# The values' scaling by the lengths of K: one VectorE instruction in the middle of a chunk step, or eight ScalarE instructions at its end

## The chip, the cores and the metric

One core of one Trainium2 chip runs the whole program. The metric is the device time of one execution in microseconds (us). Three runs of the kernel before are at hand, and one further execution with the profiler on, from which all rows below are taken.

## What is computed

Three stages follow one another: linear attention with the delta rule over 4 x 8 heads of 768 tokens and 48 features, then a mixture of 8 experts over 3072 tokens, then a gated feed-forward layer. The change lies in the first stage.

```python
k_n = k / (norm(k, axis=-1) + 1e-06)
for t in range(S):
    y[:, :, t] = einsum('bhd,bhde->bhe', q[:, :, t], state)
    v_old = einsum('bhde,bhd->bhe', state, k_n[:, :, t])
    state = state + beta[:, :, t] * einsum('bhd,bhe->bhde', k_n[:, :, t], v[:, :, t] - v_old)
```

## The kernel before

The attention works in 24 chunk steps (NSTEP) of 32 tokens, all 32 heads at once: 128 partitions hold 4 batches x 32 tokens, and the 8 heads lie along the free axis. Four steps make a group g, so there are six groups. K is used unnormalized in two products, and to make up for that the values V of a step are multiplied by the lengths of K, which stand in `nt` (one number per partition and head). `v_mul` (L203) does that in place on the tile VT, two steps ahead of the use; from step 1 on it is called with VectorE (L893). Steps 0 to 2 got theirs from GpSimd earlier.

In a step TensorE's work stands in this order: KS (the state read with K), Y's first half (the state read with Q), U (a triangular inverse times W), XTP (transposes of the step before for the gate of the experts), 24 of the 32 matmuls GP (K with K and Q with K, eleven steps ahead, only while there are such steps, s <= 12), Sps (the new state), Y's second half, GL (the gate), and the last 8 of GP. Between them stand these hand-overs: VectorE makes W from VT and KS (L804); U waits for W; ScalarE copies U to UH in half precision (L830), VectorE subtracts that to get the low half (L834); Sps waits for UH, behind its first 16 of 48 matmuls also for the low half; ScalarE copies Sps to SH, from which the next step's KS is read.

ScalarE's queue at a step's end holds: the evacuation XG of Y (L502), in every second step a cast PHL (L291), the copies G and P of GP (L272), then `kh_mul` (L301, eight activations ks, one per head, each with a column of `rnt` as its scale, in the form that the changed `v_mul` has too), in every second step the two casts KH (L314), in some steps a zeroing of X, and then, in the next step, two copies of the inverse into TBD (L401) in four steps of the attention, and UH.

VectorE has besides a background work: for every group the inverse of a 32x32 triangular matrix per head is made column by column (tiles X, tmp, Lt), and ends with a transpose XT and the copies into TBD. An object `Filler` (L96) deals this work out while the program is written. It keeps a clock of its own, and `run(budget)` (L123) places background instructions until the budget is used up; `spend(dur)` (L129) moves the clock on by what other VectorE work takes, so that less background work is placed. Each step has a budget of TA = 3.4 between U and UH and TB = 6.8 at its end (TC = 5.8 once s + 1 + LA >= NSTEP, with LA = 11). The transpose XT of group g + 1 may come from step 4g on (`limit`, L837). The engines' queues keep the order of the program (class Queue, L75): an instruction that waits holds up all behind it on its engine.

Where this text says step s, it means the stretch from UH of step s to UH of step s + 1, and W(s), U(s), UH(s) are the instructions of step s.

Of the kernel before, what the change touches and what calls it, by code (L numbers as in the profile page):

```python
# [12 lines left out]
AF = mybir.ActivationFunctionType  # L13
# [8 lines left out]
NSTEP, NG = SEQ // CH, SEQ // CH // 4  # L22
# [119 lines left out]
class Attention:  # L142
# [5 lines left out]
    def run(self, small, acc, zero_fill, small_loads):  # L148
        tc, a, beside = self.tc, self.a, self.beside
        nc = tc.nc  # L150
        V, A, G = [Queue(tc, e) for e in (nc.vector, nc.scalar, nc.gpsimd)]
# [15 lines left out]
        nt = cp.tile([128, NG, 32], F32, name="nt")  # L167
# [35 lines left out]
        def v_mul(s, E=G):  # L203
            g, s4 = divmod(s, 4)
            norms(g)
            v = VT[s // 2][:, s % 2].rearrange("p (h e) -> p h e", h=8)
            E.tensor_tensor(out=v, in0=v, in1=nt[:, g, 8 * s4 : 8 * s4 + 8].unsqueeze(2).to_broadcast([128, 8, 48]), op=ALU.mult)


# [2 lines left out]
        def gp_mm(s, hs, mm=T.matmul):  # L212
            if s not in GPS:
                tag = {4: "KS", 5: "Y", 7: "XTP", 8: "GL", 9: "U"}.get(s, "GP")
                GPS[s] = pool(tag).tile([128, 8, 64], F32, tag=tag, name="GP", bufs=1)
            ps, t = GPS[s], KT[s]
            for h in hs:
                for p in range(2):
                    mm(out=ps[64 * p : 64 * p + 64, h], lhsT=KB[s % RK][0:112, p, :, h], rhs=t[0:112, :, p, :, h], start=True, stop=True)
# [45 lines left out]
        def gp_evac(s):  # L265

            ps = GPS.pop(s)
            KT.pop(s)
            g, s4 = divmod(s, 4)
            if s4 == 0 and g > 0:  # L270
                GPM[g] = [ep.tile([128, 32, 32], F32, tag=n, name=n, bufs=b) for n, b in (("G", 2), ("P", 2))]
            A.copy(out=GPM[g][0][:, 8 * s4 : 8 * s4 + 8], in_=ps[:, :, 0:32])  # L272
            return A.copy(out=GPM[g][1][:, 8 * s4 : 8 * s4 + 8], in_=ps[:, :, 32:64]).ins
# [4 lines left out]
        def p_split(u, E=G):  # L278
            g, i = divmod(u, 2)
            if g:  # L280
                norms(g)
                pm = GPM[g][1][:, 16 * i : 16 * i + 16]
                E.tensor_tensor(out=pm, in0=pm, in1=rnt[:, g, 16 * i : 16 * i + 16].unsqueeze(2).to_broadcast([128, 16, 32]), op=ALU.mult)
            else:
                pm = PM.pop(u)
            E.tensor_tensor(out=pm, in0=pm, in1=mask.unsqueeze(1).to_broadcast([128, 16, 32]), op=ALU.mult)
            PHL[u] = wk.tile([128, 2, 16, 32], F16, tag="PHL", name="PHL", bufs=4)
            PMS[u] = pm
# [7 lines left out]
        def expand(dst, src):  # L296
            for b in range(4):
                SP.dma_start(out=dst[32 * b : 32 * b + 32, :, :, b].rearrange("p a k i -> p (a k) i"), in_=src[32 * b : 32 * b + 32].rearrange("p a k i -> p (a k) i"))


        def kh_mul(u, half=None):  # L301
            norms(u // 2)
            r = rnt[:, u // 2].rearrange("p (s h) -> p s h", s=4)
            if u not in KS_N:
                KS_N[u] = wk.tile([128, 2, 8, 48], F32, tag="ks", name="ks", bufs=1)
            for i in (range(2) if half is None else (half,)):
                for h in range(8):
                    A.activation(out=KS_N[u][:, i, h], in_=KTOK[u][:, i, :, h], func=AF.Copy, scale=r[:, 2 * (u % 2) + i, h : h + 1])

        def kh_split_hi(u):  # L310
            KTOK.pop(u)
            KH = wk.tile([128, 2, 2, 8, 48], F16, tag="KH", name="KH", bufs=1)
            for s in range(2):
                A.copy(out=KH[:, s, 0], in_=KS_N[u][:, s])  # L314
            KHG[u] = KH
# [67 lines left out]
        def norms(g):  # L383
            while g not in normed:
                fil.step()
# [112 lines left out]
        def x_evac(s, Yp):  # L498
            if s % 2 == 0:
                XGP[s // 2] = gs.tile([128, 2, ROW], F32, tag="XG", name="XG", bufs=4)  # L500
            XG[s] = XGP[s // 2][:, s % 2]
            A.activation(out=XG[s][:, 0:384], in_=fl(Yp), func=AF.Copy, scale=1.0 / SIG)  # L502
# [98 lines left out]
        def scatter(s):  # L601
            g, s4 = divmod(s, 4)
            pos, sc = GT[g]
            x = XG.pop(s)
            G.tensor_copy(out=x[:, 384:386], in_=sc[:, s4])
            r = G.indirect_dma_start(out=self.disp, out_offset=bass.IndirectOffsetOnAxis(ap=pos[:, s4 : s4 + 1], axis=0), in_=x, in_offset=None)
            if s >= NSTEP - 8:

                tc.declare_no_dep(r.ins, group=f"rows{g}", reason="each token has a row of its own")
                tc.add_to_no_dep_group(f"rows{g}", r.ins)  # L610
# [26 lines left out]
        fil = Filler()  # L637
# [49 lines left out]
        for ops in prep(0):  # L687
            flush(ops)
        v_mul(0)

        def ahead(s):
# [55 lines left out]
        gp_evac(10)  # L747
        kh_split_lo(1)
        v_mul(1)
        p_split(1)  # L750
        W = wk.tile([128, 8, 48], F32, tag="W", name="W", bufs=1)
# [27 lines left out]
        for s in range(NSTEP):  # L779
            g, s4 = divmod(s, 4)  # L780
# [108 lines left out]
            if s == NSTEP - 2:  # L889
                for w in range(NSTEP - 8, NSTEP - 4):  # L890
                    scatter(w)
            if s + 2 < NSTEP and s:
                v_mul(s + 2, V)  # L893
                fil.spend(0.48)
            x_evac(s, Yp)
            if s > 4 and s4 == 1:
                fil.flush(v1)
# [12 lines left out]
            if more and s:  # L910
                gp_mm(s + LA, H8[GS:], mm)
                gp_evac(s + LA)
            if s == 0:
                expand(PBD[1], PHL.pop(1))
                kh_mul(2, 0)
                p_split(2)
                v_mul(2)
            elif half and s4 != 3:
                kh_mul(u + 2, s2)
                if s2:  # L920
                    kh_split_hi(u + 2)
# [630 lines left out]
```

## Time and profile before

| | us |
|---|---|
| median of three runs | 1078.68 |
| lowest and highest of them | 1072.25 and 1078.94 |
| the profiled execution | 1077.86 |
| its span, first to last instruction | 1076.2 |

The span is the stretch in which instructions are recorded; 1.7 us of the execution lie around it. Engines are named PE (TensorE's matmuls), PEld (its weight loads), DVE (VectorE), ACT (ScalarE), POOL (GpSimd), SP (the queue that issues most transfers). In a row of the timeline the first number is the start, the second the time, and in brackets stands for how long the engine had been idle and what it waited for. A row of the waits has the time in all, how often, and the longest. The attention's steps run from about 62 to 350 us.

### The profile page before, as it was taken

The page shows a single profiled execution, that of the slowest core. Times are in us where ns is not written, and L with a number is a line of the kernel's source. Part 1 is how long each engine was busy: PE and PEld are TensorE (multiplying, and loading weights), DVE is VectorE, ACT ScalarE, POOL GpSimd, SP SyncE. Part 2 cuts the span into 40 slices and gives each one's busy share as a digit, 9 for nine tenths or more (in the row PEclk, how much of TensorE's full clock was granted, in tenths as well). Part 3 has the DMA queues.
Part 4 walks back from the last instruction along what each step waited for, and adds up shares of the span by engine and source line. Part 5 has one row for each costly group of instructions (what it writes and reads, how often), then busy time and mean ns, then how long its engine had stood idle before and what let it go on. Part 6 is the DMA issues. An engine that isn't in the chain of part 4 may idle for free. (4 is left out here: it accounts for less than half of the span.)

```text
span 1076.2 us, 22516 instructions
## 1 busy us (share of the span) xinstructions
PE 1016.2 (94%) x9111; PEld 919.6 (85%) x9112; DVE 547.4 (51%) x1498; ACT 397.2 (37%) x880; POOL 313.5 (29%) x304
## 2 busy tenths in 40 slices
PE   9778899997999999999889999999999999999997
PEld 8678888887889988788889988888888888888886
DVE  6968899999534577666683374511211211211211
ACT  6634545464443454454445322221212222212111
POOL 8520002102011234445443234332322311321322
PEclk9887577655565999999999999999999999999999
DMA  7999978654574365555544122000000000000000
GB/s 193 204 182 245 150 162 160 156 93 103 105 158 127 112 214 155 159 152 178 163 126 129 22 85 74 23 23 1 23 8 1 30 1 1 30 1 1 30 1 30
DMA packets 178366, 102.47 MB, mean 95 GB/s; under 512 B 126841, under 2 KB 166722, under 8 KB 178258
## 3 DMA queue, kind: packets, MB, share of 16 engines
q1 hardware_dynamic: 175186, 91.53, 35.8%
q0 software_dynamic: 3072, 9.46, 2.4%
q8 instruction: 73, 1.20, 0.5%
q14 instruction: 35, 0.29, 0.1%
HBM read 74.94 MB, written 15.80 MB: 84 GB/s over the span
## 5 line engine op out<-in xcount | busy, mean ns | idle before, releaser
L1473 DVE TENSOR_TENSOR gf<-gf,g 128x512 f32<-128x512 f32 x72 | 49.5, 688 | 308.9 <-PE g L1465 308.3
L975 POOL TENSOR_TENSOR gsl<-gf,gsh 128x512 fp32r<-128x512 f32 x68 | 88.5, 1302 | 270.1 <-ACT gsh L974 270.1
L1472 ACT ACTIVATE gf<-g 128x512 f32<-128x512 f32 x72 | 43.0, 598 | 184.5 <-PE g L1465 184.0
L974 ACT CAST gsh<-gf 128x512 fp32r<-128x512 f32 x69 | 42.8, 620 | 145.7 <-DVE gf L1473 145.1
L1439 PE MATMUL o<-woh,gsl 128*128 128x384 f32 x272 | 87.2, 338 | 0.0
L1439 PE MATMUL o<-wol,gsh 128*128 128x384 f32 x272 | 86.5, 337 | 0.0
L87 DVE TENSOR_TENSOR X<-X,tmp 128x84 f32<-128x84 f32 (+37 forms) x303 | 74.2, 275 | 0.8
L87 DVE TENSOR_TENSOR tmp<-X,Lt 128x84 f32<-128x84 f32 (+37 forms) x303 | 73.9, 274 | 1.4
L1155 DVE SCALAR_TENSOR_TENSOR hl<-h,hh 128x460 fp32r<-128x460 f32 (+7 forms) x57 | 33.1, 581 | 62.7 <-ACT hh L1154 62.6
L1114 PE MATMUL y<-hh,w2h 128*128 128x460 f32 (+6 forms) x168 | 60.9, 362 | 2.2 <-ACT hh L1154 2.1
L1465 PE MATMUL g<-yl,wgh 128*128 128x512 f32 x216 | 62.6, 395 | 0.0
L1465 PE MATMUL g<-yl,wvh 128*128 128x512 f32 x216 | 62.3, 395 | 0.0
L87 POOL COPY XG<-g_sc 128x2 f32<-128x2 f32 x24 | 6.0, 248 | 192.9 <-DVE g_sc L87 152.5
L1439 PE MATMUL o<-woh,gsh 128*128 128x384 f32 x272 | 61.7, 337 | 0.0
L1465 PE MATMUL g<-yh,wgh 128*128 128x512 f32 x180 | 60.9, 395 | 0.0
L87 PE MATMUL U<-W,TBD 64*64 64x48 f32 x768 | 42.0, 282 | 18.2 <-DVE W L87 11.3
L87 ACT ACTIVATE ks<-kth,rnt 128x48 f32<-128x48 f32 x192 | 54.5, 371 | 11.3 <-DMA kth<-in_ktok_dram 11.3
L1114 PE MATMUL y<-hh,w2l 128*128 128x460 f32 (+6 forms) x168 | 58.6, 349 | 0.0
L87 PEld LDWEIGHTS U<-W,TBD 64*64 64x64 f32 x768 | 38.3, 197 | 21.0 <-DVE W L87 12.6
L87 PE MATMUL GP<-KT,KB 112*64 112x64 f32 x640 | 47.7, 314 | 8.8 <-DMA KB<-in_st_dram 7.6
L1439 PEld LDWEIGHTS o<-woh,gsh 128*128 128x128 f32 x272 | 49.7, 188 | 5.8
L87 PEld LDWEIGHTS GP<-KT,KB 112*64 112x64 f32 x640 | 42.6, 221 | 13.2 <-POOL KH L87 6.5
(335 smaller groups left out, 2406.5 us busy)
## 6 DMA issues: line engine op xcount, KB each, us to landing
w1r<-in_w_dram SPq DMA_DIRECT2D x32, 384.0 KB
w2r<-in_w_dram SPq DMA_DIRECT2D x32, 384.0 KB
KT<-in_st_dram SPq DMA_DIRECT2D x20, 448.0 KB
disp<-TBD SPq DMA_DIRECT2D x8, 772.0 KB
kth<-in_ktok_dram SPq DMA_DIRECT2D x12, 384.0 KB
VT<-in_vtok_dram SPq DMA_DIRECT2D x12, 384.0 KB
KBD<-KH SPq DMA_DIRECT2D x48, 96.0 KB
XG<-in_m2g_dram SPq DMA_DIRECT2D x12, 384.0 KB
```

Source lines behind the costliest of these rows:

```text
L87: r = f(*args, **kw)
L974: (act or nc.scalar).copy(out=hi, in_=src)
L975: eng.tensor_tensor(out=lo, in0=src, in1=hi, op=ALU.subtract)
L1114: self.T.matmul(out=ys[c][:, 0:n], lhsT=w2[l][:, f % 2, 128 * c : 128 * c + 128], rhs=(hh, hl)[r], start=(f == 0 and i == 0), stop=(f == 7 ...
L1155: self.V.scalar_tensor_tensor(out=hl, in0=hp[:, 0:n], scalar=0.0, in1=hh, op0=ALU.max, op1=ALU.subtract)
L1439: T.matmul(out=ops_[m][:, 0:384], lhsT=gh[l][:, 128 * m : 128 * m + 128], rhs=wo[r][:, f], start=(f == 0 and i == 0), stop=(f == 11 and i ...
L1465: T.matmul(out=ps, lhsT=gv[w][l][:, c, 128 * f : 128 * f + 128], rhs=Y[r][c], start=(i == 0 and c == 0), stop=(i == 2 and c == 2))
L1472: A.activation(out=gf, in_=gps[0], func=AF.Sigmoid)
L1473: V.tensor_tensor(out=gf, in0=gf, in1=gps[1], op=ALU.mult)
```

## The change

`v_mul` gets a branch for ScalarE, which multiplies head by head. Its call in the step's middle goes, with the 0.48 that the Filler's clock was moved on for it; a call with ScalarE stands now behind GP's evacuation and ahead of `kh_mul`. Steps 0 to 2 keep theirs on GpSimd; 21 calls move.

```diff
             v = VT[s // 2][:, s % 2].rearrange("p (h e) -> p h e", h=8)
+            if E is A:
+                for h in range(8):
+                    A.activation(out=v[:, h], in_=v[:, h], func=AF.Copy, scale=nt[:, g, 8 * s4 + h : 8 * s4 + h + 1])
+                return
             E.tensor_tensor(out=v, in0=v, in1=nt[:, g, 8 * s4 : 8 * s4 + 8].unsqueeze(2).to_broadcast([128, 8, 48]), op=ALU.mult)
...
-            if s + 2 < NSTEP and s:
-                v_mul(s + 2, V)
-                fil.spend(0.48)
             x_evac(s, Yp)
...
                 gp_evac(s + LA)
+            if s + 2 < NSTEP and s:
+                v_mul(s + 2, A)
             if s == 0:
```

The order in which the instructions stand changes with it. On ScalarE, from the end of step 12 to UH(13) (G and P are the evacuations of GP, ks is `kh_mul`, TBD_107 is the tile of the next inverse), there stands before:

```order
L87 ACTIVATE XG<-Y 128x384
L87 COPY G<-GP 128x256
L87 COPY P<-GP 128x256
L87 ACTIVATE ks<-kth,rnt 128x48 x8
L87 ACTIVATE X<-X 128x1024
L87 COPY TBD_107<-XT 32x8x32 x2
L87 CAST UH<-U 128x384
```

and now:

```order
L87 ACTIVATE XG<-Y 128x384
L87 COPY G<-GP 128x256
L87 COPY P<-GP 128x256
L87 ACTIVATE VT<-VT,nt 128x48 x8
L87 ACTIVATE ks<-kth,rnt 128x48 x8
L87 ACTIVATE X<-X 128x1024
L87 COPY TBD_107<-XT 32x8x32 x2
L87 CAST UH<-U 128x384
```

Eight activations on VT came in between P and ks; nothing else moved on this engine in that step.

On VectorE, the end of the inverse of group 2 (its last column X 128x31, the transpose XT, the copies into TBD_107) stands before right ahead of UH(6):

```order
L87 TENSOR_TENSOR tmp<-X,Lt 128x31
L87 TENSOR_TENSOR Lt<-Lt,bx 128x8x24
L87 TENSOR_TENSOR X<-X,tmp 128x31
L87 TENSOR_TENSOR Lt<-Lt,bx 128x16x16
L87 STREAM_TRANSPOSE XT<-X 128x32x32
L87 COPY TBD_107<-XT 32x8x32 x2
L87 TENSOR_TENSOR UH<-U,UH 128x384
```

and now right ahead of W(6):

```order
L87 TENSOR_TENSOR tmp<-X,Lt 128x31
L87 STREAM_TRANSPOSE nt<-by 128x32
L87 TENSOR_TENSOR X<-X,tmp 128x31
L87 TENSOR_TENSOR Lt<-Lt,bx 128x256
L87 STREAM_TRANSPOSE XT<-X 128x32x32
L87 COPY TBD_107<-XT 32x8x32 x2
L87 SCALAR_TENSOR_TENSOR W<-VT,KS 128x384
```

The transpose and the copies have moved from the stretch behind W(6) to the stretch ahead of it.

On VectorE again, in the last inverse, that of group 5, the rows from UH(15) on (PHL is the low half made by `p_split_lo`; the rows with tmp and X are the inverse's columns) stand before as

```order
L87 TENSOR_TENSOR UH<-U,UH 128x384
L87 TENSOR_TENSOR P<-P,rnt 128x512
L87 TENSOR_TENSOR P<-P,mask 128x512
L87 TENSOR_TENSOR VT<-VT,nt 128x384
L87 TENSOR_TENSOR tmp<-X,Lt 128x100
L87 TENSOR_TENSOR tmp<-X,Lt 128x120
L87 TENSOR_TENSOR X<-X,tmp 128x10x10
L87 TENSOR_TENSOR X<-X,tmp 128x12x10
L87 TENSOR_TENSOR PHL<-P,PHL 128x512
L87 TENSOR_TENSOR tmp<-X,Lt 128x90
L87 TENSOR_TENSOR tmp<-X,Lt 128x117
```

and now as

```order
L87 TENSOR_TENSOR UH<-U,UH 128x384
L87 TENSOR_TENSOR P<-P,rnt 128x512
L87 TENSOR_TENSOR P<-P,mask 128x512
L87 TENSOR_TENSOR tmp<-X,Lt 128x80
L87 TENSOR_TENSOR tmp<-X,Lt 128x112
L87 TENSOR_TENSOR X<-X,tmp 128x10x8
L87 TENSOR_TENSOR X<-X,tmp 128x14x8
L87 TENSOR_TENSOR tmp<-X,Lt 128x70
L87 TENSOR_TENSOR tmp<-X,Lt 128x105
L87 TENSOR_TENSOR X<-X,tmp 128x10x7
L87 TENSOR_TENSOR X<-X,tmp 128x15x7
L87 TENSOR_TENSOR PHL<-P,PHL 128x512
```

The multiplication of VT is gone, and two columns of the inverse (those that begin with 128x100 and 128x90) are done before UH(15).

## Rows read from the trace of the kernel before

**Rows 1.** The page: VectorE's busy tenths and TensorE's granted clock, 40 slices of 26.9 us.
```profile
DVE  6968899999534577666683374511211211211211
PEclk9887577655565999999999999999999999999999
```

**Rows 2.** Steps 4, 7, 10, 13, 17: length, busy (instructions) PE, PEld, DVE, ACT, POOL, PEclk, DMA, GB/s.
```profile
121.42:133.69 12.27, 12.27 (x216) 11.55 (x217) 11.74 (x41) 6.17 (x16) 0.00 (x0) 0.52 0.83 118
...
158.72:171.53 12.81, 11.10 (x216) 10.40 (x217) 12.61 (x54) 6.55 (x18) 4.08 (x4) 0.84 0.89 176
...
196.78:209.30 12.52, 12.52 (x216) 11.77 (x217) 12.45 (x61) 5.22 (x15) 3.50 (x5) 0.50 0.80 177
...
233.65:249.08 15.43, 10.38 (x189) 9.69 (x190) 14.24 (x69) 6.26 (x18) 2.13 (x4) 0.56 0.37 80
...
283.43:294.14 10.71, 10.71 (x189) 10.00 (x190) 4.72 (x17) 6.26 (x19) 1.35 (x3) 0.50 0.47 83
```

**Rows 3.** What TensorE waited for from 60 to 345 us.
```profile
PE U L87 <- DVE W L87: 11.3, 7, 3.8
...
PE Sps L87 <- ACT UH L87: 5.4, 3, 4.0
PE Sps L87 <- DVE UH L87: 2.7, 4, 1.2
```

**Rows 4.** The tiles VT and ks: durations in ns (lowest/median/highest).
```profile
L87 DVE TENSOR_TENSOR VT<-VT,nt x21: 526/551/553, 82.9 to 325.4; 128x384 f32<-128x384 f32 x21
...
L87 ACT ACTIVATE ks<-kth,rnt x192: 362/370/395, 27.2 to 310.4; 128x48 f32<-128x48 f32 x192
```

**Rows 5.** What ScalarE waited for before UH, 80 to 340 us.
```profile
ACT UH L87 <- PE U L87: 65.0, 19, 7.7
```

**Rows 6.** ScalarE's timeline at UH(5), UH(7) and up to UH(13).
```profile
133.69 0.48 ACT L87 CAST UH<-U 128x384 f16<-128x384 f32 x1 [1.71 <-PE U L87]
...
158.72 0.48 ACT L87 CAST UH<-U 128x384 f16<-128x384 f32 x1 [1.92 <-PE U L87]
...
229.31 2.27 ACT L87 ACTIVATE ks<-kth,rnt 128x48 f32<-128x48 f32 x8
231.48 1.05 ACT L87 ACTIVATE X<-X 128x1024 uint32<-128x1024 uint32 x1
232.54 0.81 ACT L87 COPY TBD<-XT 32x256 f32<-32x256 f32 x2
233.65 0.48 ACT L87 CAST UH<-U 128x384 f16<-128x384 f32 x1 [0.29 <-PE U L87]
```

**Rows 7.** TensorE's timeline at Sps of step 13, U of step 14 and U of step 16.
```profile
235.91 1.29 PE L87 MATMUL Sps<-UH,KBD 64*128 64x48 f16 x32 [1.18 <-DVE UH L87]
...
247.09 1.95 PE L87 MATMUL U<-W,TBD 64*64 64x48 f32 x32 [3.77 <-DVE W L87]
...
271.10 1.95 PE L87 MATMUL U<-W,TBD 64*64 64x48 f32 x32 [2.98 <-DVE W L87]
```

**Rows 8.** VectorE's timeline: the inverse's end behind W(6), then step 15 up to W(16).
```profile
145.85 2.24 DVE L87 STREAM_TRANSPOSE XT<-X 128x1024 f32<-128x1024 f32 x1
148.12 0.58 DVE L87 COPY TBD<-XT 32x256 f32<-32x256 f32 x2
...
262.90 0.55 DVE L87 TENSOR_TENSOR VT<-VT,nt 128x384 f32<-128x384 f32 x1
263.37 0.45 DVE L87 TENSOR_TENSOR tmp<-X,Lt 128x100 f32<-128x100 f32 x2
...
264.51 0.69 DVE L87 TENSOR_TENSOR PHL<-P,PHL 128x512 f16<-128x512 f32 x1 [0.33 <-ACT PHL L87]
265.12 0.44 DVE L87 TENSOR_TENSOR tmp<-X,Lt 128x90 f32<-128x90 f32 x2
...
265.83 0.42 DVE L87 TENSOR_TENSOR tmp<-X,Lt 128x80 f32<-128x80 f32 x2
...
270.50 0.54 DVE L87 SCALAR_TENSOR_TENSOR W<-VT,KS 128x384 f32<-128x384 f32 x1
```

## The prediction

> **What bounds the kernel now.** I read the page first: VectorE is nearly always busy in the slices 3 to 9 (some 80 to 270 us), and in the same stretch the granted clock hovers between the two levels, half of full speed (1.2 GHz) and full speed (2.4 GHz) [rows 1]. That is the attention; behind it VectorE is mostly idle, and the change touches nothing there. So what the change is worth has to be read from some 20 steps of 10 to 15 us.
>
> Next the busy times step by step [rows 2]. In steps 4 and 10 TensorE has no gap at all: 12.27 of 12.27 and 12.52 of 12.52 us, at the low level (0.52 and 0.50). There it is the bound itself, and an unburdened VectorE gains nothing. In step 7, at 0.84, its same 216 matmuls took 11.10 us of 12.81, and VectorE with 12.61 us of work was the bound. In step 13, with fewer matmuls, TensorE was busy for 10.38 of 15.43 us and VectorE for 14.24. So the two engines take turns.
>
> Then what TensorE waited for [rows 3]: U for W on VectorE 11.3 us in 7 waits, Sps for the low half of UH on VectorE 2.7 us, for ScalarE's UH 5.4 us. The first two, 14.0 us, are all that a faster VectorE could give at an unchanged clock. Two of the waits for W are more than half of the 11.3: 3.77 at U(14) and 2.98 at U(16) [rows 7].
>
> **The change, part by part.** *Removed:* 21 multiplications of VT at 0.551 us [rows 4], 11.6 us of VectorE's time. But the Filler loses 0.48 of its clock's advance per call at the same time, and so places as much more background work in that step; from the start of the multiplication to that of the next instruction passed 262.90 to 263.37, 0.47 us [rows 8]. As long as there is background work, a step's VectorE queue stays as long as it was. What is gained appears where an inverse runs out earlier, and an inverse can't be used earlier than its step. Counted in the order of the changed kernel, with the lengths of like rows, steps 1 to 4 differ by at most 0.3 us each; I count them at nothing.
>
> *Steps 5 to 8.* The inverse of group 2 now ends ahead of W(6), not behind it. The transpose and its two copies took from 145.85 to 148.70, 2.85 us [rows 8]; less the multiplication (0.47) and some 0.4 of other rows that leave the stretch, W(6) is late by 2.0 us. The same 2.85 us no longer stand between W(6) and UH(6). Over the stretches from W(5) to W(9) the rows add up to 0.5 us less than before. TensorE gets back by step 8 what it lost at step 6: I take -0.2 us for the four steps.
>
> *Added on ScalarE:* eight activations of 128x48 with a column of scales per call. The trace of before has no such activation on VT; the nearest row is ks, the same form, at 0.370 us [rows 4], and eight of them in a row took 2.17 us from their start to the next instruction (229.31 to 231.48) [rows 6]. Bounds: 2.17, if they overlap as those do, and 8 x 0.370 = 2.96 if they did not. I take 2.17, since ks is the nearest row in every respect. Over 21 calls that is 45.6 us of ScalarE. It lies where ScalarE waited for U anyway: 65.0 us in 19 waits, 3.4 us each on average [rows 5]. Behind the eight stand, on the same engine, ks, KH, the zeroing of X, the copies into TBD and at last UH, for which VectorE and Sps wait. Where the wait before UH was under 2.17, UH is late: by 0.46 at UH(5) and 0.25 at UH(7) (1.71 and 1.92 of waiting) [rows 6]. There U is followed on TensorE by XTP and 24 matmuls GP, so that nothing waits; without that cover it would be these 0.7 us.
>
> *Step 13* is the one without cover. The copies into TBD ended at 232.54 + 0.81 = 233.35, 0.29 us before UH [rows 6]. With 2.17 more they end at 235.5, UH's high half comes at 236.0 and VectorE's low half, 0.55 later, at about 236.6; Sps' last 32 matmuls started at 235.91 [rows 7]. GP is at its end there, only XTP lies between. So 0.7 us, and VectorE's queue up to W(14), which ends last there, starts 0.7 us later and has 0.3 us more rows: W(14) is late by 1.0 us. The wait of 3.77 does not get shorter.
>
> *Steps 14 to 16.* The last inverse uses up all that is left of the gain, for its end lies right ahead of W(16) and nothing follows. In step 15 the multiplication goes and two columns of the inverse are done before UH(15): from 262.90 to 264.51, less 0.33 of waiting, are 1.28 us, and from 265.12 to 265.83 another 0.71 [rows 8], together 2.0. Steps 14's rows give a further 0.4. W(16) is ready 2.4 us sooner after W(14) than it was. Behind W(16) VectorE waits for TensorE (4.72 us busy of 10.71 in step 17 [rows 2]), and its 0.55 per step are worth nothing.
>
> *Sum:* -0.2 + 1.0 - 2.4 = -1.6 us. The profiled execution took 1077.86, which becomes 1076.3; it stands 0.8 below the median of the three runs, so 1077.1 is the time that I name.
>
> *Hidden at no cost:* VT's load is issued a step ahead and no wait for it is recorded, and the multiplication now comes later than it did; the transfer of the next kth waits for ks to be read, 2.17 us later, and is issued by SP ahead of the rest of TBD, which is needed a step later, some 10 us.
>
> **Rivals.** *ScalarE becomes the bound (slower).* For it: 2.17 us exceed the wait before UH in three of the steps named. UH(5) and UH(7) lie where the clock goes up to the full level: step 7 needed 11.10 us at 0.84 for what step 10 needed 12.52 for at 0.50 [rows 2], so a step wholly at full speed is worth 1.42 x 0.50 / 0.34 = 2.1 us. If late UHs open gaps there, TensorE stays low. The page's digits over 5 in slices 3 to 7 (2, 0, 2, 2, 1) [rows 1] make 0.7 / 0.5 x 26.9 = 38 us at the full level, some 3.3 steps, 7.0 us in all; with 0.46 + 0.25 + 1.87 of direct lateness and no gain, 9.6 us slower: 1088.3. It decides from the point where ScalarE's queue ends later than U by more than XTP and GP cover, about 1.7 us. Against it: the two overhangs are 0.46 and 0.25.
>
> The Trainium skill speaks for this rival (ScalarE: Activation LUTs, section "Rules for kernel authors": multiplications belong on VectorE, not ScalarE). The rows agree on the price, four times the time here; whether the time counts hangs on the waits named above, and by the rule alone the time would be this rival's.
>
> *VectorE's time counts in full (faster).* If the fill were no more than a shift, all 11.6 us would come back: 1066.3, by the median 1067.1. For it: steps 7 and 13. Against it: steps 4 and 10, where TensorE has no gap, and that the last steps don't need VectorE.
>
> *The Filler gives nothing back (the change doesn't do what it says).* W(6) stays 2.0 late, step 13 costs its 1.0, and what W(16) gains is lost because TensorE is not there sooner: 3.0 us slower, 1081.7 by the median. Against it: 2.98 us of wait at U(16), which W alone sets.
>
> **Numbers.** Forecast 0.55; ScalarE bound 0.13; VectorE in full 0.14; nothing given back 0.18. A measurement of this kernel tells about 1% from no change, 10.8 us; the three runs alone spread over 6.7. The second rival lies at that edge, so a little over half of its chance is faster, 0.08; of the first, which lies just short of it, and with activations at 2.96 instead of 2.17, 0.08 slower; the rest, 0.84, is no change. The range reaches to both rivals and takes in the clock's turns: 1067 to 1087.
>
> **What would show it.** Right: the eight activations on VT start to start about 0.27 us apart; VectorE's busy time 11 to 12 us lower; the wait at U(16) down from 2.98 to near 1; the wait at U(14) still over 3; a wait of Sps for ScalarE's UH in step 13; a new wait of about 2 us at U(6). Wrong: waits of Sps for ScalarE's UH in most steps (first rival), or steps 7 to 10 shortened by half a microsecond each (second), or a granted clock that stays at one level through steps 9 to 19, which nothing in this working can foresee.

## The result and the profile after

The changed kernel took 1082.18 us (median of 20 runs), the one before on the same chip 1077.9 (20 runs): ratio 1.0056, 95% interval 1.0032 to 1.0081. The two medians stand 4.3 us apart, the ratio says some 6 us slower, where 1.6 us faster was forecast. A second measurement on another chip (below) gave 1.0072. The profiled execution of the changed kernel took 1083.84 us with a span of 1082.1, 5.9 more than before. Of two kernels below, g_none and b_spend, the execution profiled was a disturbed one, so that their ratios are used and not their profiles (the 1.47 and 1.15 us that one expectation below quotes are g_none's).

Where the 5.9 us arose is read from the starts of UH on ScalarE, the marks between the steps. The changed kernel reaches UH(8) 3.7 us ahead of the one before; 1.4 of that stood already at UH(0), ahead of the first call that moved. Then step 8 takes 3.8 us more (17.98 against 14.19), step 9 3.2 more (14.28 against 11.06), step 12 3.1 more (14.72 against 11.67) and step 16 2.4 more (12.76 against 10.34); steps 13 to 15 together take 2.6 less, and the rest behind UH(8) differs by 0.1 in all. At UH(23) it is 6.05 us late. Four steps out of 23 hold the loss, 12.5 us, of which about half is made up elsewhere.

Busy time by step, for steps 8, 9, 12 and 16 of the changed kernel (columns as in [rows 2]):

```profile
167.85:185.83 17.98, 11.08 (x216) 10.42 (x217) 13.55 (x54) 8.75 (x26) 1.01 (x1) 0.81 0.86 147
185.83:200.11 14.28, 12.96 (x221) 12.06 (x222) 11.88 (x58) 8.78 (x29) 1.37 (x3) 0.50 0.45 101
225.52:240.24 14.72, 12.63 (x216) 11.81 (x217) 9.92 (x26) 8.78 (x27) 0.00 (x0) 0.50 0.60 104
277.06:289.82 12.76, 10.45 (x184) 9.74 (x185) 6.31 (x15) 7.22 (x24) 0.00 (x0) 0.50 0.61 103
```

The same four steps of the kernel before:

```profile
171.53:185.72 14.19, 13.65 (x242) 12.73 (x242) 13.62 (x51) 6.98 (x18) 2.86 (x1) 0.67 0.93 168
185.72:196.78 11.06, 9.61 (x200) 9.09 (x197) 9.68 (x45) 6.88 (x21) 1.45 (x3) 0.90 0.62 145
221.98:233.65 11.67, 11.67 (x216) 10.99 (x217) 11.08 (x33) 6.96 (x19) 0.00 (x0) 0.56 0.64 104
273.09:283.43 10.34, 10.34 (x184) 9.70 (x185) 6.52 (x16) 5.38 (x15) 0.00 (x0) 0.50 0.52 104
```

In steps 12 and 16 before, TensorE had no gap (11.67 of 11.67, 10.34 of 10.34); now it stands for 2.1 and 2.3 us. In step 8 it stands for 6.9 us, and no engine is busy for the whole step, so the next question is who waits for what. In step 9 the matmuls themselves take longer, at 0.50 where they had 0.90.

UH is a mark on ScalarE, and ScalarE can itself be late. In the kernel before, UH(9) started 1.87 us after U(9) had ended, behind copies into TBD that had waited for XT; in the changed kernel it started at once. So the border between steps 8 and 9 has moved (TensorE's 242 and 200 matmuls became 216 and 221). From one start of U to the next, TensorE's own mark, the four steps take 17.12 us against 13.11, 14.34 against 12.14, 14.65 against 12.49 and 12.69 against 10.34: 4.0, 2.2, 2.2 and 2.4 more. From U(9) to U(10) the work is the same, in the kernel before and in the changed one:

```profile
182.65:194.79 12.14, 10.69 (x221) 10.04 (x221) 10.66 (x42) 7.68 (x22) 0.64 (x2) 0.99 0.68 172
183.78:198.12 14.34, 13.03 (x221) 12.12 (x221) 11.77 (x61) 8.16 (x27) 1.37 (x3) 0.50 0.40 94
```

The matmuls' 2.3 us more, at the lower of the two levels, are all that this step lost.

What TensorE waited for from 60 to 355 us in the changed kernel (against [rows 3]):

```profile
PE U L87 <- DVE W L87: 15.3, 9, 4.0
PE U L87 <- DMA TBD<-XT: 6.9, 4, 4.1
PE U L87 <- DMA QB<-in_st_dram: 6.7, 1, 6.7
PE Sps L87 <- DVE UH L87: 0.8, 3, 0.4
...
PE Sps L87 <- ACT UH L87: 0.6, 1, 0.6
```

The third row is a trap: it names a transfer into QB. TensorE's timeline and VectorE's show that W(9) ended at 183.21 + 0.52 = 183.73, and U(9) started 0.05 later; in the second profile of the same kernel the same wait, 5.05 us, is put down to W. So the waits for W are 22 us, not 15.3, against 11.3 before.

TensorE's timeline at U(6), U(9), U(13), U(14), U(16) and U(17):

```profile
144.33 1.94 PE L87 MATMUL U<-W,TBD 64*64 64x48 f32 x32 [2.52 <-DVE W L87]
...
183.78 2.01 PE L87 MATMUL U<-W,TBD 64*64 64x48 f32 x32 [6.74 <-DMA QB<-in_st_dram]
...
238.18 2.02 PE L87 MATMUL U<-W,TBD 64*64 64x48 f32 x32 [2.09 <-DVE W L87]
...
253.06 1.94 PE L87 MATMUL U<-W,TBD 64*64 64x48 f32 x32 [4.03 <-DVE W L87]
...
275.07 1.94 PE L87 MATMUL U<-W,TBD 64*64 64x48 f32 x32 [0.85 <-DVE W L87]
...
287.76 1.51 PE L87 MATMUL U<-W,TBD 64*64 64x48 f32 x23 [2.31 <-DVE W L87]
```

And why was W late? VectorE's own waits have a group that the kernel before does not have at all, 11.0 us in 3 waits; in VectorE's timeline these are the transposes XT in steps 8, 12 and 16 (with W(9)):

```profile
177.94 2.00 DVE L87 STREAM_TRANSPOSE XT<-X 128x1024 f32<-128x1024 f32 x1 [3.80 <-DMA TBD<-XT]
183.21 0.52 DVE L87 SCALAR_TENSOR_TENSOR W<-VT,KS 128x384 f32<-128x384 f32 x1
...
231.19 2.22 DVE L87 STREAM_TRANSPOSE XT<-X 128x1024 f32<-128x1024 f32 x1 [3.66 <-DMA TBD<-XT]
...
282.57 2.25 DVE L87 STREAM_TRANSPOSE XT<-X 128x1024 f32<-128x1024 f32 x1 [3.50 <-DMA TBD<-XT]
```

XT is the transposed inverse; its tile has one buffer (`bufs=1`). When a group's first step is reached, `expand_rest` (L407 of the changed kernel) has SP issue four transfers that read XT and spread it into TBD. The transpose of the next inverse writes the same buffer and must wait until they have read it; W stands behind the transpose on VectorE, U waits for W. SP's queue in the changed kernel, at the loads of kth and these transfers (start, time of issuing):

```profile
169.04 1.20 SPq L87 DMA_DIRECT2D kth<-in_ktok_dram  x1
170.60 3.49 SPq L87 DMA_DIRECT2D TBD<-XT  x4
...
224.01 0.35 SPq L87 DMA_DIRECT2D kth<-in_ktok_dram  x1
224.41 3.12 SPq L87 DMA_DIRECT2D TBD<-XT  x4
...
274.61 0.35 SPq L87 DMA_DIRECT2D kth<-in_ktok_dram  x1
275.01 3.11 SPq L87 DMA_DIRECT2D TBD<-XT  x4
```

From the first issue to the start of the transpose that waited for it are 7.3, 6.8 and 7.6 us. In the kernel before the same distances were there to be read, and nothing waited yet:

```profile
172.31 3.72 SPq L87 DMA_DIRECT2D TBD<-XT  x4
...
219.33 3.12 SPq L87 DMA_DIRECT2D TBD<-XT  x4
...
267.79 3.06 SPq L87 DMA_DIRECT2D TBD<-XT  x4
```

and VectorE's transposes, the first right behind W(9):

```profile
182.09 0.51 DVE L87 SCALAR_TENSOR_TENSOR W<-VT,KS 128x384 f32<-128x384 f32 x1
182.75 2.10 DVE L87 STREAM_TRANSPOSE XT<-X 128x1024 f32<-128x1024 f32 x1
...
226.38 2.16 DVE L87 STREAM_TRANSPOSE XT<-X 128x1024 f32<-128x1024 f32 x1
...
275.48 2.06 DVE L87 STREAM_TRANSPOSE XT<-X 128x1024 f32<-128x1024 f32 x1
```

10.4, 7.1 and 7.7 us: in steps 12 and 16 there was little to spare (in f_bnospend below, 6.6 and 6.1 us were still enough). The change eats it from both sides. The Filler, with 0.48 less on its clock per call, places the transpose sooner, in step 8 even ahead of W(9). And ScalarE's eight new instructions delay ks, for whose reading the load of kth waits, and the transfers stand behind that load on SP: counted from UH(12), their first issue moved from 2.65 us ahead of it to 1.1 ahead, while VectorE was ready for the transpose 2.0 us behind it instead of 4.4. In step 16 it is nearly all the transfers: 5.3 us ahead of UH(16) became 2.05, and the transpose came 0.4 sooner.

Two views speak against ScalarE itself being the trouble. The new instructions take little, and the time that ScalarE waited for U (80 to 340 us) fell from the 65.0 of [rows 5] to 34.6:

```profile
L87 ACT ACTIVATE VT<-VT,nt x168: 317/324/350, 85.7 to 335.8; 128x48 f32<-128x48 f32 x168
```
```profile
ACT UH L87 <- PE U L87: 34.6, 20, 5.0
```

### The profile page after: what moved, and what is told of

Its sections match the earlier page's. It is cut to its first block, busy times and chain, and to the rows that moved or that the text cites. A ratio compares the mean times of both kernels' runs of the same rounds, so it can differ in the third digit from the quotient of the medians.

```text
span 1082.1 us, 22679 instructions
## 1 busy us (share of the span) xinstructions
PE 1021.1 (94%) x9111; PEld 923.0 (85%) x9112; DVE 540.4 (50%) x1485; ACT 435.6 (40%) x1048; POOL 313.2 (29%) x304
## 5 line engine op out<-in xcount | busy, mean ns | idle before, releaser
L87 DVE TENSOR_TENSOR X<-X,tmp 128x150 f32<-128x150 f32 (+33 forms) x307 | 75.9, 278 | 0.7
L87 DVE TENSOR_TENSOR tmp<-X,Lt 128x150 f32<-128x150 f32 (+33 forms) x307 | 75.0, 276 | 1.4
L87 PE MATMUL U<-W,TBD 64*64 64x48 f32 x768 | 44.0, 288 | 28.9 <-DVE W L87 15.3
```

What stands on the lines that cost most here:

```text
L87: r = f(*args, **kw)
```

## The experiments

**Theory:** XT's single buffer makes the loss, on two routes: the Filler's shift (steps 8 and 9) and the later transfers behind ScalarE's work (steps 12 and 16). **Rivals:** ScalarE's time itself; the lower granted clock alone; the Filler's new order without the buffer. In all, twelve kernels; ratios are to the kernel before on the same chip.

| kernel | Filler's 0.48 kept | ScalarE multiplies | buffers of XT | ratio | 95% interval |
|---|---|---|---|---|---|
| after, after_again | no | yes | 1 | 1.0056, 1.0072 | 1.0032 to 1.0081, 1.0029 to 1.0115 |
| a_xt2 | no | yes | 2 | 0.9984 | 0.9949 to 1.0019 |
| b_spend | yes | yes | 1 | 0.9988 | 0.9946 to 1.0030 |
| m_spendxt2 | yes | yes | 2 | 0.9970 | 0.9941 to 0.9999 |
| g_none | no | nobody does | 1 | 1.0033 | 1.0001 to 1.0064 |
| f_bnospend | no | no (VectorE) | 1 | 1.0040 | 1.0015 to 1.0064 |
| p_nospendxt2 | no | no (VectorE) | 2 | 0.9997 | 0.9978 to 1.0016 |
| e_bxt2 | yes | no (VectorE) | 2 | 0.9977 | 0.9951 to 1.0003 |

### The changed kernel again, and with a second buffer

> The changed kernel once more, beside the others of this call. Both theories: 1.003 to 1.008 of before, with waits of VectorE before XT for the transfers of TBD at steps 8, 12 and 16, 9 to 12 us in all. If the waits are not there a second time, or the ratio is under 1.002, the first profile was an accident of one execution and the cause is open again.

1085.96 us, ratio 1.0072. The three waits for XT are there again (4.19, 4.08 and 2.29 us), and step 9 again took 14.27.

```diff
-                XT = wk.tile([128, 32, 32], F32, tag="XT", name="XT", bufs=1)
+                XT = wk.tile([128, 32, 32], F32, tag="XT", name="XT", bufs=2)
```

> The changed kernel with two buffers for the tile XT instead of one. Theory 1 (the Filler, whose clock no longer advances by 0.48 per call, brings each transpose XT earlier in VectorE's queue, where it has to wait until the transfers that copy the previous XT into TBD have read it; W(9), W(13), W(17) stand behind it): the 11.0 us in which VectorE waits before XT for TBD's transfers go, the waits of U(9) 6.74, U(13) 2.09 and U(17) 2.31 fall under 1 us each, and the time falls by 4 to 8 us against the changed kernel, to 1074 to 1078. Theory 2 (ScalarE's eight activations per step make everything behind them late, at whatever buffer): no fall, 1081 to 1083. Theory 3 (the clock's turns alone): no fall beyond 2 us.

1074.52 us, ratio 0.9984: one number undoes the loss. No wait for XT is left; U(9) waits 1.18 us, a little more than expected, U(13) and U(17) not at all. Steps 8, 12 and 16:

```profile
171.44:185.23 13.79, 12.61 (x216) 11.78 (x217) 13.13 (x49) 8.79 (x26) 0.59 (x1) 0.50 0.92 166
222.72:235.91 13.19, 12.17 (x218) 11.31 (x219) 10.31 (x29) 8.78 (x26) 0.00 (x0) 0.60 0.68 135
272.40:282.74 10.34, 10.34 (x184) 9.70 (x185) 6.12 (x15) 7.18 (x23) 0.00 (x0) 0.50 0.81 152
```

In the changed kernel they took 17.98, 14.72 and 12.76: 8.1 us together, for 7.3 of span. Step 12 is still longer than before (11.67) because UH(13) is late by ScalarE's queue; from U(12) to U(13) it takes 12.51 us, where it was 12.49. Step 9 stayed at 14.27, so its loss is not the long wait's.

### Each route alone

The Filler's shift alone: the kernel before, only without its 0.48.

```diff
-                fil.spend(0.48)
```

> The kernel before with nothing changed but the Filler's advance of 0.48 per call, which is left out; VectorE goes on multiplying VT, ScalarE has no new work. Theory 1: the transposes come earlier in the order, though VectorE has 0.55 us more per step than in the changed kernel; a wait before XT of 1.5 to 4 us at step 8, under 2 at steps 12 and 16, and 1.001 to 1.005 of before. If ScalarE's late ks is needed for any of it: no wait before XT and 0.998 to 1.002.

1083.61 us, ratio 1.0040. VectorE still multiplies and ScalarE does nothing new, and yet step 8 has the whole wait, and only step 8. VectorE's timeline at the three transposes, and TensorE's at U(9):

```profile
183.25 1.97 DVE L87 STREAM_TRANSPOSE XT<-X 128x1024 f32<-128x1024 f32 x1 [3.90 <-DMA TBD<-XT]
...
231.27 2.03 DVE L87 STREAM_TRANSPOSE XT<-X 128x1024 f32<-128x1024 f32 x1
...
280.44 2.07 DVE L87 STREAM_TRANSPOSE XT<-X 128x1024 f32<-128x1024 f32 x1
```
```profile
189.06 2.02 PE L87 MATMUL U<-W,TBD 64*64 64x48 f32 x32 [7.29 <-DMA QB<-in_st_dram]
```

Steps 8 and 9 took 32.8 us (25.25 before), steps 12 and 16 11.77 and 10.33, as before (11.67, 10.34). So the wait in step 8 needs the Filler's shift alone, and those in steps 12 and 16 need ScalarE's part as well.

The same with the second buffer:

> The kernel before (VectorE multiplies, nothing on ScalarE), only without the 0.48 of the Filler's clock, and with two buffers for XT. It parts the Filler's shift from the wait that the shift runs into. Theory (the shift costs because XT comes up against the transfers that read it): no wait for XT, the wait of 7.3 us at U(9) gone down to about 1, steps 8 and 9 together about 28 us against 32.8 with one buffer, ratio 0.996 to 1.001. Rival (the shift costs by itself, for W(9) then stands behind XT on VectorE and TensorE goes through step 9 at its low clock): steps 8 and 9 at 30 us or more, ratio 1.002 to 1.005.

Ratio 0.9997, steps 8 and 9 28.5 us, U(9) waits 1.59: as the theory had it. The shift costs 3.2 us in these steps even without the wait: 1.0 from U(8) to U(9) (14.16 against 13.11), where W(9) stands behind XT and its copies, and 2.2 from U(9) to U(10), where the granted clock is 0.50, as the rival had it. Steps 13 to 15 give 2.2 back (37.2 us, 39.4 in the kernel before).

The other side: the changed kernel with the Filler's 0.48 kept.

```diff
+            if s + 2 < NSTEP and s:
+                fil.spend(0.48)
             x_evac(s, Yp)
```

> The changed kernel with the Filler's advance of 0.48 kept where it stood, so that VectorE's instructions stand in the order of before without the 21 multiplications, and ScalarE has its eight activations. Theory 1: XT stands behind W(9) again and hardly waits (under 3 us in all, at steps 12 and 16 where ScalarE delays the transfers), the waits for W shrink below the 11.3 us of before, 1073 to 1077. Theory 2: still 1081 to 1083, with waits of Sps for ScalarE's UH over 3 us in all.

Ratio 0.9988: with the old order ScalarE's 168 instructions cost nothing that can be measured, though XT has one buffer. So the loss needs the shift; ScalarE's part only adds to it.

The eight instructions left out on every engine:

```diff
-            if s + 2 < NSTEP and s:
-                v_mul(s + 2, A)
```

> The changed kernel with the calls of v_mul in the steps left out on every engine: the values of steps 3 to 23 stay unscaled. VectorE's order is that of the changed kernel, ScalarE's that of before. Theory 1: the wait before XT stays, 8 us or more in all, and the time stays at 1079 to 1083, although no engine does the work. Theory 2: without ScalarE's share the time falls to 1075 or below.

Ratio 1.0033 (1.0001 to 1.0064). The median, 1078.04 us, lies between the two expectations and so decides for neither. The values behind the attention are other ones here, which makes the time of the later stages a weaker comparison. Slower than before all the same, with 21 multiplications less on any engine: a lighter VectorE does not help while the order runs into the buffer. Against the changed kernel's 1.0056 and 1.0072 the intervals overlap, so ScalarE's share of the loss is not settled by the times; that it has one is seen in the waits of steps 12 and 16.

### Moving what stands ahead of the transfers

The load of kth issued behind them on SP:

```diff
-                if half:
-                    load_kth(u + 2)
...
                 expand_rest(g)
...
+            if s2 == 0 and 0 < s < NSTEP - 2 and half:
+                load_kth(u + 2)
```

> The changed kernel with the load of kth issued behind the transfers of the rest of TBD instead of ahead of them, so that these do not wait for ScalarE to read the last kth. If the wait before XT comes from ScalarE's lateness by way of this load: the 11.0 us fall to 5 or less and the time by 3 to 5 us. If it comes from XT's earlier place (theory 1): 8 us or more of the 11.0 stay, above all the 3.8 at step 8, and the time falls by 0 to 2 us.

Ratio 1.0005 (0.9971 to 1.0040). The waits in steps 12 and 16 are gone (the steps took 13.22 and 9.67 us), that in step 8 stayed, at 2.90 us. This is the second route, shown from SP's side by the waits; the interval of the ratio still meets the changed kernel's.

The same from ScalarE's side, the multiplication behind ks and KH:

```diff
-            if s + 2 < NSTEP and s:
-                v_mul(s + 2, A)
...
+            if s + 2 < NSTEP and s:
+                v_mul(s + 2, A)
```

> The changed kernel with the eight activations on VT behind ks and KH at the very end of the step, so that the load of kth, and behind it on SP the transfers of TBD, find ks done as early as before. If the waits at steps 12 and 16 come by way of the load of kth (theory 1 with its second part): they fall from 3.7 and 3.5 to 1 to 2 each, as they were with no scaling at all (1.47 and 1.15), and the one at step 8 stays at 2.5 to 4, for it comes from the Filler; the time is 1.000 to 1.004 of before. If ScalarE's work as such is the cause, whatever stands behind it: all three waits stay over 3 and the time stays at 1.004 or more.

Ratio 1.0013 (0.9986 to 1.0040): VectorE waits before XT for these transfers 3.97 us in step 8, 1.15 in step 12 and not at all in step 16; step 12 took 13.19 us, step 16 9.50. With ks as early as before, 2.5 of the 3.66 us in step 12 are gone and all of the 3.50 in step 16. The 1.15 us left in step 12 do not come by way of ks.

### What is the relief of VectorE worth, and is there more?

The kernel before with the second buffer alone, and the changed one with both mendings:

> The kernel before with two buffers for XT. The trace of before has no wait before XT, so theory 1 expects no difference: 0.998 to 1.002 of before. If the second buffer helps by itself (another place in memory, another order), it falls as much as the changed kernel did with it, and the fall there is no evidence.

> The changed kernel with both mendings: the Filler's advance of 0.48 kept in its place, and two buffers for XT. No wait before XT; VectorE's order as before without the 21 multiplications. If VectorE's relief is worth something once nothing gives it back: 0.992 to 0.997 of before, that is 3 to 9 us. If TensorE at its low clock bounds the steps (the bound of my forecast): 0.997 to 1.000.

0.9977 and 0.9970, by intervals the same. So the change itself, freed of its accident, is worth nothing that can be measured; U waited 11.2 us for W in m_spendxt2, where it was 11.3 before. The kernel before fell a little more with the buffer than expected (0.9977, with 1 still in its interval), so some 0.0023 of the changed kernel's fall from 1.0056 to 0.9984 may be the buffer's own; the rest is the wait's. m_spendxt2 is the only version here whose interval lies below 1 (1071.43 us), and only just.

With kth's load moved as well:

> The changed kernel with the Filler's advance kept, two buffers for XT, and the load of kth behind TBD's transfers. Nothing should wait before XT, and nothing is gained over the two mendings alone, since with two buffers no wait hangs on these transfers: 0.994 to 0.999 of before. If the earlier transfers of TBD were worth something by themselves (U waiting for TBD): below 0.994.

1079.86 us, ratio 1.0008 (0.9979 to 1.0037): a miss. It has none of the waits for XT, and its interval meets that of m_spendxt2; whether the moved load costs something is open.

The multiplication on GpSimd, from the kernel before with two buffers:

```diff
-                v_mul(s + 2, V)
+                v_mul(s + 2)
```

> The kernel before with two buffers for XT and the multiplication on GpSimd at its old place, the Filler's advance kept. VectorE and ScalarE are both free of it. If VectorE's relief is worth nothing once the buffer is there: the same as the kernel before with two buffers, 0.995 to 1.000. If what keeps the changed kernel from gaining is ScalarE's load: 0.990 to 0.995.

1088.25 us, ratio 1.0084 (1.0057 to 1.0110), a clear miss. The waits of U for W are 16.8 us, with 5.01 at U(14). VectorE's timeline around one multiplication, and GpSimd's:

```profile
248.26 0.41 DVE L87 TENSOR_TENSOR X<-X,tmp 128x28 f32<-128x28 f32 x2
248.60 1.10 DVE L87 TENSOR_TENSOR tmp<-X,Lt 128x27 f32<-128x27 f32 x2
249.62 1.01 DVE L87 TENSOR_TENSOR X<-X,tmp 128x27 f32<-128x27 f32 x2
...
251.21 0.55 DVE L87 SCALAR_TENSOR_TENSOR W<-VT,KS 128x384 f32<-128x384 f32 x1
```
```profile
248.40 1.01 POOL L87 DMA_INDIRECT disp<-XG,g_pos  x1 [0.59 <-POOL XG L87]
249.44 0.94 POOL L87 TENSOR_TENSOR VT<-VT,nt 128x384 f32<-128x384 f32 x1
```

Two pairs of the kind that takes 0.41 us alone take 1.10 and 1.01 beside GpSimd's two instructions. W(14) stands two such pairs behind them. That this is where the whole loss comes from was not tried.

## Why the prediction was wrong, and where it was right

**The step that failed** is "Hidden at no cost": kth's load, 2.17 us later, "is issued by SP ahead of the rest of TBD, which is needed a step later, some 10 us". I had the delay and what is queued behind it, and asked only who needs what the transfers write (TBD, for U). I did not ask who waits for what they read. XT has one buffer, and the next transpose was due 7.1 and 7.7 us behind their issue; in the changed kernel they need 6.8 to 7.6. These rows were in the trace of before and I did not look them up. Costs, from U to U: 2.2 us in step 12 and 2.4 in step 16, where the sum had nothing; with a second buffer both are gone (12.51 and 10.34).

**The second failure**, from the same omission, is the term of -0.2 us for steps 5 to 8. Steps 5 to 7 took 0.8 us less, near it; step 8 took 3.8 more. The working followed the order of the changed kernel, in which the transpose stands ahead of W(9), but added up rows with their old lengths, and no row of before carried the wait. Step 9 had no term at all: 2.2 us from U(9) to U(10), all of it the granted clock's. The first rival had worked out what the clock is worth in a step, 2.1 us, and was near it; why the clock was low there stays open.

The measured time lies inside the stated range and close to the 1081.7 us of the rival "The Filler gives nothing back". That is chance: what this rival takes for lost, the gain at W(16), did come, and what the kernel lost stood in no term of the sum and in no rival.

**Right in sign and size:** the sign expected at U(6), a wait of about 2 us, came (2.52, where 0.95 had been). U(14) kept its wait (3.77, now 4.03), and that of U(16) fell from 2.98 to 0.85. From U(14) to U(16) it is 22.0 us instead of 24.0, for the 2.4 expected. Most of that is the Filler's shift and not VectorE's relief: f_bnospend, where VectorE still multiplies, has 22.5, and m_spendxt2, where it doesn't but the 0.48 is kept, 24.5.

**Step 13** was forecast 1.0 late with Sps waiting for ScalarE's UH. In the changed kernel UH(13) came to wait 1.54 us for U instead, since U(13) was itself late. Where the buffer's wait is gone the mechanism shows: in a_xt2 Sps waited 1.55 us for UH(13), in m_spendxt2 0.44, with ScalarE's queue without a gap up to UH(13). Its price was smaller than the 1.0: from U(13) to U(14) it is 15.15 and 15.02 us in these two, 14.62 in the kernel before and 15.40 in e_bxt2, where ScalarE has no new work.

**ScalarE's price** was set too high: 1.82 us from the first multiplication to the first ks (245.28 to 247.10), 0.23 each, where ks gave 2.17 in all. That it is hidden was right but for step 13, and b_spend's ratio says so. Sps waited 0.6 us for ScalarE's UH, where it was 5.4 [rows 3], but by itself this proves little: U was late, and in a_xt2, where it was not, it is 5.4 again. The rival "ScalarE becomes the bound" foresaw the right side for the wrong reason, and with it the rule of the Trainium skill (ScalarE: Activation LUTs, section "Rules for kernel authors") that speaks for VectorE: the price is more than three times VectorE's here (1.82 against 0.55 us), and b_spend shows that it does not count.

**VectorE's busy time** fell from 547.4 to 540.4 us in all, less than the 11 to 12 expected; from 60 to 355 us it fell from 222.92 to 212.21, 10.7.

## What to carry to other kernels

When an instruction is moved, ask of every transfer behind it both who waits for what it writes and who waits for what it reads; a tile with one buffer that is read by a transfer is a deadline, and the distance from the issue to the next write, read from the old trace, less what the transfers need, is the slack. A planner's clock is part of the change: 0.48 us less on it per call made the kernel 0.4% slower by itself (f_bnospend). A step's length hangs on the mark that it is read from: read it on the engine that the question is about. Where an engine was made lighter and nothing came of it, try the cheap mending (here one buffer) before the work is moved back.

## What the runs showed of the hardware that was not expected

- **Step 9 follows the granted clock, and not the wait.** From U(9) to U(10) TensorE has the same work in every kernel here, 220 or 221 matmuls. Where the granted clock was 0.99 or 1.00, the matmuls took 10.7 us and the stretch 12.1 to 12.2 (the kernel before, e_bxt2, m_spendxt2, o_poolxt2); at 0.50 they took 13.0 and the stretch 13.8 to 14.3. All seven profiles without the Filler's 0.48 that are used here have 0.50. But the long wait at U(9) is not needed for it (a_xt2, with 1.18 us there), nor is the missing 0.48 (n_all, which keeps it). These two:

```profile
183.18:197.51 14.33, 13.02 (x220) 12.12 (x220) 11.75 (x61) 9.57 (x30) 1.36 (x3) 0.50 0.58 140
181.11:194.94 13.83, 13.01 (x221) 12.11 (x221) 10.18 (x41) 9.63 (x30) 0.82 (x2) 0.50 0.69 159
```

Between UH(8) and U(9) the clock had been 0.57 in the kernel before and rose; it had been 0.86 in the changed kernel, where TensorE then stood for 6.7 us, and 0.50 in a_xt2 and n_all, where it stayed. What decides between the two is not settled.
- **A lower granted clock is no verdict on a version.** n_all's profiled execution had 0.884, as the changed kernel's, with a span 7.3 us shorter.
- **VectorE was slower beside GpSimd:** pairs of 0.41 us took 1.0 to 1.1 us beside its instructions. The 0.94 us that GpSimd's own multiplication takes doesn't show this price. This is read from one trace and was not tried by itself.
